# Relus, memory rows and tile values at other steps and engines in a fused chunk attention and feed-forward kernel

## The chip, the cores and the metric

The kernel runs on one core of a Trainium2 chip. Time is device time in microseconds (us). The kernel before was timed six times: the median is 212.51 us, the runs lie between 211.23 and 214.04 us.

## The reference, cut to what matters

Attention goes over chunks of 32 queries; each chunk sees 16 keys to its left, its own 32, 8 to its right, and 8 memory rows. Its output is normalised and goes through a two-layer perceptron with a residual.

```python
# q, k, v: (4, 8, 768, 64); mem_k, mem_v: (4, 8, 8, 64)
for c in range(24):                                   # chunks of 32
    k_ctx = k[:, :, max(0, 32*c - 16) : min(768, 32*c + 40)]
    k_full = concat([mem_k, k_ctx]); v_full = concat([mem_v, v_ctx])
    a = softmax(scale * q_c @ k_full.T)
    out[:, :, c_start:c_end] = a @ v_full
x = out.transpose(0, 2, 1, 3).reshape(4, 768, 512)
xn = (x - mean(x)) / sqrt(var(x) + 1e-6) * g_ln       # over the 512
y = x + maximum(xn @ w_ch1, 0) @ w_ch2                # 512 -> 2048 -> 512
```

## The kernel before, in words

**Tiles and units.** A tile is 128 rows of `x` (one batch has six, there are 24). Three tiles make a unit: units 0 and 1 hold batch 0, units 2 and 3 batch 1 and so on, counted in the tiles of the perceptron. The perceptron of unit `u` runs while the attention of the next unit's tiles is made.

**Steps.** A unit has 28 steps, written out by the loop at lines 901 to 923. In steps 0 to 15, `up` multiplies the three turned tiles `xT` by one 128-wide slice `hc` of the first weight (four matmuls of 384 columns) into one of four PSUM buffers `mm`, which rotate; a relu then moves it to `rT`. Line 435 says on which engine: for units 2 to 7 (`PAIRED`) VectorE takes `hc` 3, 5, 8, 11, 13 and 15, ScalarE the rest. In steps 16 to 27, `down` and `paired` multiply `rT` by the second weight. In units 2 to 7, `down` makes the third tile in steps 16 to 19 and `finish` (line 483) empties its `mm` buffer; `paired` makes the first two tiles from sums and differences of blocks, which VectorE prepares in `mixed_r` (lines 503 to 512, operation at line 491). The fourth product of `paired` goes into the buffer that `finish` empties.

**What is planned beside it.** `at(u, step, fn, ...)` puts other work behind the perceptron's work of a step. An engine takes its instructions in the order in which they are written; there is no other scheduler. `attend` plans three attention tiles: `scores` (line 326) and `soften` (the exponential on ScalarE, line 337), then `weigh` (probabilities by values, line 354), `gather` (VectorE, lines 363 to 373, divides and takes the mean), `norm` (line 376) one step later, `turn_x` (two or more steps later) and `stats` (line 381, ScalarE). Tiles listed in `ON_PE` are turned by four TensorE transposes and a VectorE copy (lines 404 and 409), the others by a DMA transpose on SyncE's queue (line 399).

**Memory rows.** `v_mem` (line 142) copies the eight memory value rows of a batch to the partitions 96 to 103 of the value buffer `V`, four groups at a time. For batches 2 and 3 ScalarE does it at steps 17, 21 and 24 of units 1 and 3.

**Loads.** GpSimd's queue starts nearly all loads, in the order of the program: the values of unit 0 between quarters of the first weight (`w1c`) and of the second (`w2c`), lines 659 to 687. `mix` (line 304) is a VectorE copy of a landed block of keys or queries (`st` to `iv`), which is then turned by TensorE (batches 0 and 1) or by DMA (`cross`, batches 2 and 3) and put in its place by `spread`. Unit 0 begins as a written-out list (lines 697 to 767) and goes on with the steps from 10.

Of the kernel before, what the change touches and what calls it, by code (L numbers as in the profile page):

```python
# [15 lines left out]
def kernel(  # L16
# [20 lines left out]
    GW = 4 * W  # L37
    VW = 80
    HD = 65
    ON_PE = (0, 1, 2, 3, 4, 5, 8)  # L40
    NEG = -30000.0

    ctx.enter_context(tc.manual_schedule())
# [43 lines left out]
    def slot(kind):  # L87
        lst = {"att": att, "mm": mm}[kind]
        turn[kind] = (turn[kind] + 1) % len(lst)
        return lst[turn[kind]]  # L90
# [4 lines left out]
    def free(ap, off, pattern, parts=None):  # L95
        p = list(ap.ap[0]) if parts is None else [ap.ap[0][0], parts]
        return bass.AP(tensor=ap.tensor, offset=ap.offset + off, ap=[p] + [list(x) for x in pattern])

    def as16(t):
        return t.bitcast(FP16)  # L100

    def copy(eng, out, in_):
        if eng is nc.scalar:
            eng.copy(out=out, in_=in_)  # L104
        else:
            eng.tensor_copy(out=out, in_=in_)  # L106

    dve, act, pool = nc.vector, nc.scalar, nc.gpsimd
    ring = {}

    def pick(lst, key):
        key = (id(lst),) + key
        if key not in ring:
            ring[key] = ring.setdefault(("n", id(lst)), 0) % len(lst)
            ring[("n", id(lst))] += 1
        return lst[ring[key]]
# [168 lines left out]
    def mix_q(b, blk, half, eng):  # L285
        rows = slice(64 * half, 64 * half + 64)
        s, o = pick(st, ("b", b, blk, 1))[rows, :], pick(iv, ("b", b, blk, 1))[rows, :]
        copy(eng, free(o, 0, [[64, 2], [128, 8], [1, 64]]), s)
# [13 lines left out]
    def mix(b, blk, which, eng):  # L302
        s, o = pick(st, ("b", b, blk, which)), pick(iv, ("b", b, blk, which))
        copy(eng, free(o, 0, [[64, 2], [128, 8], [1, 64]]), s)
# [40 lines left out]
    def values(b, t):  # L345
        weigh(b, t)
        gather(b, t)

    def weigh(b, t):
        p = value_slot[b, t] = slot("att")  # L350
        for par in range(2):
            for j in range(4):
                for gg in range(2):
                    nc.tensor.matmul(  # L354
                        out=p[64 * gg : 64 * gg + 64, par, 128 * j : 128 * j + HD],
                        lhsT=AT[t % 3][:, par, gg, j, :],
                        rhs=V[b % 2][:, 2 * t + gg, 4 * par + j, 0:HD],
                        start=(j == 0), stop=(j == 3), tile_position=(0, 64 * gg),
                    )

    def gather(b, t):
        p, r, x = value_slot[b, t], rec[t % 2], xs[(NT * b + t) % 9]
        nc.vector.reciprocal(out=r, in_=free(p, 64, [[128, 8]]))  # L363
        nc.vector.scalar_tensor_tensor(  # L364
            out=x.rearrange("p (h d) -> p h d", h=8),
            in0=free(p, 0, [[128, 8], [1, 64]]), scalar=1.0,
            in1=free(r, 0, [[1, 8], [0, 64]]),
            op0=ALU.mult, op1=ALU.mult, accum_out=tot[t],
        )
        nc.vector.tensor_scalar(  # L370
            out=nmean[t], in0=tot[t], scalar1=-1.0 / 512, scalar2=None, op0=ALU.mult
        )

    def norm(b, t, gb=gb):
        i = NT * b + t
        nc.vector.scalar_tensor_tensor(  # L376
            out=xn[i % 4], in0=xs[i % 9], scalar=nmean[t], in1=gb, op0=ALU.add, op1=ALU.mult,
        )
# [16 lines left out]
    def turn_x(b, t):  # L395
        i = NT * b + t
        dst = xT[(i // 3) % 2][:, :, 128 * (i % 3) : 128 * (i % 3) + 128]
        if i not in ON_PE:
            nc.sync.dma_start_transpose(out=dst, in_=xn[i % 4])
            return  # L400
        p = slot("att")
        pv = as16(p[:, 0, :])
        for dt in range(4):
            nc.tensor.matmul(
                out=pv[:, 128 * dt : 128 * dt + 128],
                lhsT=xn[i % 4][:, 128 * dt : 128 * dt + 128], rhs=identity,
                is_transpose=True, start=True, stop=True,
            )
        nc.vector.tensor_copy(out=dst, in_=free(pv, 0, [[128, 4], [1, 128]]))
# [10 lines left out]
    def relu(eng, o, p):  # L420
        if eng is nc.scalar:
            nc.scalar.activation(out=o, in_=p, func=ACTF.Relu)  # L422
        else:
            nc.vector.tensor_scalar(out=o, in0=p, scalar1=0.0, scalar2=None, op0=ALU.max)  # L424

    def up(u, hc, lo=0, n=3):
        p = slot("mm")[:, 0 : 128 * n]
        c, i = hc // 4, hc % 4
        for dt in range(4):
            nc.tensor.matmul(  # L430
                out=p, lhsT=free(w1c[c][:, dt, :], i, [[4, 128]]),
                rhs=xT[u % 2][:, dt, 128 * lo : 128 * (lo + n)],
                start=(dt == 0), stop=(dt == 3),
            )
        on_dve = hc in (3, 5, 8, 11, 13, 15) if u in PAIRED else hc % 2 == 0
        relu(dve if on_dve else act, rT[c][:, i, 128 * lo : 128 * (lo + n)], p)

    def up_two(u, c, engs):

        for m, eng in enumerate(engs):  # L440
            p = slot("mm")
            for k_ in range(2):
                for dt in range(4):
                    nc.tensor.matmul(
                        out=p[:, 256 * k_ : 256 * k_ + 256],
                        lhsT=free(w1c[c][:, dt, :], 2 * m + k_, [[4, 128]]),
                        rhs=xT[u % 2][:, dt, 0:256],
                        start=(k_ == 0 and dt == 0), stop=(k_ == 1 and dt == 3),
                    )
            relu(eng, rT[c][:, 2 * m : 2 * m + 2, 0:256], free(p, 0, [[256, 2], [1, 256]]))  # L450

    def up_tile(u, c, i, eng):
        p = slot("mm")
        for k_ in range(4):
            for dt in range(4):
                nc.tensor.matmul(
                    out=p[:, 128 * k_ : 128 * k_ + 128],
                    lhsT=free(w1c[c][:, dt, :], k_, [[4, 128]]),
                    rhs=xT[u % 2][:, dt, 128 * i : 128 * i + 128],
                    start=(k_ == 0 and dt == 0), stop=(k_ == 3 and dt == 3),  # L460
                )
        pair = rT[c][:, :, 128 * i : 128 * i + 128], free(p, 0, [[128, 4], [1, 128]])
        if eng is None:
            return pair
        relu(eng, *pair)
# [22 lines left out]
    PAIRED = range(2, 8)  # L488
# [269 lines left out]
    total(cnt[:, 2:3], 96, W)  # L758
    nc.vector.tensor_tensor(out=cnt[:, 1:2], in0=cnt[:, 1:2], in1=cnt[:, 2:3], op=ALU.add)
    up_tile(0, 0, 1, act)  # L760
    up_two(0, 1, (dve, act))
    values(0, 2)
    norm(0, 2)
    up_two(0, 2, (act, act))
    turn_x(0, 2)
    mix_q(0, 1, 1, dve)
    mix(0, 2, 0, dve)
    plan = {}

    def at(u, step, fn, *args):  # L770
        plan.setdefault((u, step), []).append((fn, args))
# [11 lines left out]
    def value(tiles, s1, u, also=()):  # L783
# [9 lines left out]
        for n, i in enumerate(tiles):  # L793
            b, t = divmod(i, NT)
            at(u, s1 + 1, norm, b, t)
            at(u, s1 + n + (2, 3, 4)[(i in ON_PE) + (i == 8)], turn_x, b, t)
            at(u, s1 + n + 2, stats, b, t)
# [5 lines left out]
    def attend(i, s0, s1, s2, u):  # L803

        score((i, i + 1), s0, u)
        value((i,), s1, u, (i + 2,))
        value((i + 1, i + 2), s2, u)
# [62 lines left out]
    for b in (2, 3):  # L870
        u = 2 * b - 1
        w = u - 1
        for blk in range(3):
            if b == 3 and blk == 0:
                at(w - 1, 0, pace, 0, 0)
            at(w - 1, 0 if b == 3 else 21, load_pair, b, blk)
        at(w, 0, mem_cols, b, pool)
        at(w - 1, 24, pace_x, 6 * b - 4)
        for g in range(NG):
            at(w - 1, 24 + g // 4, load_v, b, g)  # L880
        for i in range(3):
            at(w - 1, (17, 21, 24)[i], v_mem, b, 4 * i, 4 * i + 4, act)
        for blk in range(3):
            for which in range(2):
                at(w, (3, 9, 18)[blk] + which, mix, b, blk, which, dve)
                at(w, (7, 18, 23)[blk] + 3 * which, cross, b, blk, which)
        at(w, 18, spread, b, 0, dve, act)
        at(w, 27, spread, b, 1, dve, act)
        at(u, 9, spread, b, 2, dve, act)
        attend(6 * b, 2, 8, 14, u)  # L890
    for b in (1, 2, 3):
        attend(6 * b + 3, 0, 6, 12, 2 * b)

    for n in range(8):
        at(1, 16 + n, mixed_w, n % 2, n // 2)
# [5 lines left out]
    for u in range(8):  # L901
        for step in range(U):
# [9 lines left out]
            elif u == 0:  # L912
                c, i = divmod(step - 16, 3)
                down(u, i, c)
            elif u not in PAIRED:
                i, c = divmod(step - 16, 4)
# [37 lines left out]
```

## Time and profile before

| | us |
|---|---|
| median of six runs | 212.51 |
| the profiled execution's own time | 212.71 |
| its span, first to last instruction | 210.9 |
| TensorE busy in the span | 199.4 |
| VectorE busy | 157.8 |
| ScalarE busy | 123.1 |
| GpSimd busy | 107.6 |

The granted TensorE clock was 1.00 in every slice. A timeline row gives the start, the length, the engine, the line, the operation, output and input, how many instructions are merged in it, and in brackets the idle time of the engine before it with what ended that. A busy matmul row ends with the drain of its last matmul, so two rows can touch although matmuls were started late; how late shows when the starts are counted. A row of engine times by stretch gives the stretch, the busy time and the number of instructions of an engine, the granted clock, the share of the DMA engines and GB/s.

### The profile page before, as it was taken

To read this page: it belongs to the slowest core of one execution; us is meant where nothing else is said; L and a number is where in the kernel's file an instruction comes from. 1 tells how busy PE (TensorE), PEld (TensorE's weight loads), DVE (VectorE), ACT (ScalarE), POOL (GpSimd) and SP (SyncE) were. 2 spreads that over 40 slices of the span, in tenths; PEclk is the share of its full clock that TensorE was granted. 3 is DMA by queue.
4 is the path that set the end of the run, shared out by engine and by line. 5 is a ranking of instruction groups with operands and counts; after the bars stand their busy time and mean duration, and the time that the engine had idled before them with its cause. 6 is when DMAs were issued, how large, how long until landed. Compare 5 with 4: busy or idle time off the path is not lost.

```text
span 210.9 us, 5313 instructions
## 1 busy us (share of the span) xinstructions
PE 199.4 (95%) x2052; PEld 135.2 (64%) x2052; DVE 157.8 (75%) x402; ACT 123.1 (58%) x243; POOL 107.6 (51%) x187
## 2 busy tenths in 40 slices
PE   7778699999999999999999999999999999999992
PEld 2457585556665567587657766686658765777581
DVE  6878567597979948997579778995789458863663
ACT  2777368627796997625879885528850684024100
POOL 7955598979789799725884991400040012100000
PEclk9999999999999999999999999999999999999999
DMA  5999999999999999999994999388013210320012
GB/s 152 201 195 190 207 182 182 205 116 240 179 93 125 204 170 148 141 214 193 172 157 97 98 199 184 72 177 148 9 24 99 99 29 1 103 99 0 3 50 99
DMA packets 72499, 27.72 MB, mean 131 GB/s; under 512 B 60569, under 2 KB 68505, under 8 KB 72474
## 3 DMA queue, kind: packets, MB, share of 16 engines
q0 software_dynamic: 46304, 14.71, 66.1%
q1 hardware_dynamic: 26026, 12.41, 26.8%
q10 hardware_dynamic: 144, 0.26, 0.6%
q8 instruction: 16, 0.26, 0.5%
q14 instruction: 9, 0.07, 0.1%
HBM read 30.28 MB, written 6.29 MB: 173 GB/s over the span
## 4 chain that ended last, share of the span: by engine, by line
PE 62%; DVE 11%; ACT 5%; issue 2%; DVEq 0%
PE mm L430 31%; PE mm L517 13%; PE mm L474 12%; PE att L354 3%; PE att L326 3%; DVE xs L364 2%; DVE SA L491 2%; DVE xn L376 2%; ACT AT L337 2%; ACT KT L104 1%; DVE osb L483 1%; DVE osb L533 1%; ACT rT L422 1%; DVE rT L424 1%; DVE KT L106 1%
## 5 line engine op out<-in xcount | busy, mean ns | idle before, releaser
L430 PE MATMUL mm<-xT,w1c 128*128 128x384 f16 x464 | 81.4, 327 | 0.8 <-ACT rT L422 0.6
L430 PEld LDWEIGHTS <-w1c 128*128 128x128 f16 x464 | 51.1, 115 | 22.2 <-issue 1.3
L422 ACT ACTIVATE rT<-mm 128x384 f16<-128x384 f32 (+1 forms) x76 | 37.2, 502 | 37.7 <-PE mm L430 31.1
L424 DVE TENSOR_SCALAR rT<-mm 128x384 f16<-128x384 f32 (+1 forms) x49 | 27.5, 562 | 26.0 <-PE mm L430 25.3
L474 PE MATMUL mm<-w2c,rT 128*128 128x512 f16 x192 | 44.6, 380 | 0.0
L137 POOL DMA_DIRECT2D V<-in_v_dram x48 | 37.6, 795 | 4.9 <-issue 1.4
L337 ACT ACTIVATE AT<-att,band 104x512 f16<-104x512 f32 x48 | 31.6, 689 | 4.5 <-PE att L326 4.4
L387 POOL TENSOR_SCALAR veps<-sq 128x1 f32<-128x1 f32 x24 | 7.8, 325 | 45.6 <-ACT junk L381 42.9
L474 PEld LDWEIGHTS <-rT 128*128 128x128 f16 x192 | 18.2, 98 | 19.7 <-DVE rT L424 0.8
L517 PEld LDWEIGHTS <-SA 128*128 128x128 f16 x192 | 18.8, 98 | 3.0 <-issue 0.8
L381 ACT ACTIVATE junk<-xs,nmean 128x512 f16<-128x512 f32 x24 | 17.3, 721 | 5.1 <-DVE rec L363 2.1
L517 PE MATMUL mm<-T,SA 128*128 128x256 f16 x144 | 17.0, 273 | 0.4 <-DVE osb L483 0.4
L364 DVE SCALAR_TENSOR_TENSOR xs<-att,rec 128x512 f32<-128x512 f32 x24 | 16.6, 691 | 0.8
L391 POOL TENSOR_TENSOR rstd<-veps,mhalf 128x1 f32<-128x1 f32 x24 | 16.1, 672 | 2.0
L376 DVE SCALAR_TENSOR_TENSOR xn<-xs,nmean,gb 128x512 f16<-128x512 f32 x23 | 16.8, 755 | 0.3
L517 PEld LDWEIGHTS <-rT 128*128 128x128 f16 x144 | 14.1, 98 | 2.9 <-issue 0.4
L123 POOL DMA_DIRECT2D st<-in_q_dram x24 | 13.3, 567 | 2.4 <-DMA st<-in_k_dram 1.4
L129 POOL DMA_DIRECT2D st<-in_k_dram x22 | 13.3, 615 | 2.1 <-DMA w1c<-in_moe_w_ch_dram 2.0
L104 ACT COPY V<-memv 8x2560 f16<-8x2560 f16 x6 | 13.8, 2320 | 0.1
L517 PE MATMUL mm<-w2c,rT 128*128 128x256 f16 x96 | 12.4, 273 | 0.0
L106 DVE COPY iv<-st 128x1024 f16<-128x1024 f16 (+1 forms) x22 | 10.6, 495 | 1.6 <-DMA st<-in_k_dram 1.4
L354 PEld LDWEIGHTS <-AT 104*64 104x64 f16 x384 | 7.7, 111 | 6.4 <-issue 4.4
(105 smaller groups left out, 241.2 us busy)
## 6 DMA issues: line engine op xcount, KB each, us to landing
out_dram<-osb SPq DMA_DIRECT2D x23, 256.0 KB, 2.4
V<-in_v_dram POOLq DMA_DIRECT2D x40, 96.0 KB, 6.1
st<-in_k_dram POOLq DMA_DIRECT2D x22, 128.0 KB, 5.3
w1c<-in_moe_w_ch_dram POOLq DMA_DIRECT2D x4, 512.0 KB, 9.3
w2c<-in_moe_w_ch_dram POOLq DMA_DIRECT2D x4, 512.0 KB, 8.3
st<-in_q_dram POOLq DMA_DIRECT2D x28, 64.0 KB, 4.3
st<-in_q_dram POOLq DMA_DIRECT2D x8, 128.0 KB, 7.6
V<-in_v_dram POOLq DMA_DIRECT2D x8, 80.0 KB, 5.6
```

Source lines behind the costliest of these rows:

```text
L104: eng.copy(out=out, in_=in_)
L137: nc.gpsimd.dma_start(out=V[b % 2][lo:hi, g, :, 0:64], in_=dram(v, b * H * HS + (64 * g - 16 + lo) * D, [[64, hi - lo], [HS, H], [1, 64]]),)
L337: nc.scalar.activation(out=free(AT[t % 3], 32 * c, [[64, 16], [1, 32]]), in_=free(p, 4 * c, [[64, 16], [1, 4], [8, 8]], W), func=ACTF.Exp, ...
L364: nc.vector.scalar_tensor_tensor(out=x.rearrange("p (h d) -> p h d", h=8), in0=free(p, 0, [[128, 8], [1, 64]]), scalar=1.0, in1=free(r, 0, ...
L376: nc.vector.scalar_tensor_tensor(out=xn[i % 4], in0=xs[i % 9], scalar=nmean[t], in1=gb, op0=ALU.add, op1=ALU.mult,)
L381: nc.scalar.activation(out=junk, in_=xs[(NT * b + t) % 9], func=ACTF.Square, bias=nmean[t], scale=1.0, accum_out=sq[t],)
L391: nc.gpsimd.tensor_tensor(out=rstd[(NT * b + t) % 9], in0=veps[t % 3], in1=mhalf, op=ALU.pow)
L422: nc.scalar.activation(out=o, in_=p, func=ACTF.Relu)
L424: nc.vector.tensor_scalar(out=o, in0=p, scalar1=0.0, scalar2=None, op0=ALU.max)
L430: nc.tensor.matmul(out=p, lhsT=free(w1c[c][:, dt, :], i, [[4, 128]]), rhs=xT[u % 2][:, dt, 128 * lo : 128 * (lo + n)], start=(dt == 0), st ...
L474: nc.tensor.matmul(out=p, lhsT=rT[c][:, k_, 128 * i : 128 * i + 128], rhs=w2c[c][:, k_, :], start=(c == 0 and k_ == 0), stop=(c == 3 and k ...
L517: nc.tensor.matmul(out=p, lhsT=left(h)[:, k_, :], rhs=right(h)[:, k_, :], start=(h == 0 and k_ == 0), stop=(h == 1 and k_ == 3),)
```

## The change

It has five parts. (1) Tile 7 (batch 1, second tile) is turned by TensorE, at step 19 of unit 1, and no longer by DMA at step 18. (2) In units 2 to 7, VectorE takes the relus 1, 2, 4, 5, 8, 10 in even units and 3, 4, 6, 7, 10, 11 in odd ones; ScalarE has the last four or five. (3) The memory rows of batches 2 and 3 are copied by VectorE at steps 0, 1 and 2 of units 2 and 4, and no longer by ScalarE. (4) The second and third tile of an attention group are weighed one step earlier (13 for 14, 11 for 12), and with them their gathering, norm, turning and stats. (5) In unit 0, tile 2's values stand ahead of the second quarter of the first weight; both relus of that quarter are ScalarE's; the third quarter is split around tile 2's turning.

```diff
-    ON_PE = (0, 1, 2, 3, 4, 5, 8)
+    ON_PE = (0, 1, 2, 3, 4, 5, 7, 8)
...
-        on_dve = hc in (3, 5, 8, 11, 13, 15) if u in PAIRED else hc % 2 == 0
+        on_dve = hc in ((1, 2, 4, 5, 8, 10), (3, 4, 6, 7, 10, 11))[u % 2] if u in PAIRED else hc % 2 == 0
...
-        for m, eng in enumerate(engs):
+        for m, eng in engs:
...
     up_tile(0, 0, 1, act)
-    up_two(0, 1, (dve, act))
     values(0, 2)
+    up_two(0, 1, ((0, act), (1, act)))
     norm(0, 2)
-    up_two(0, 2, (act, act))
+    up_two(0, 2, ((0, act),))
     turn_x(0, 2)
+    up_two(0, 2, ((1, act),))
     mix_q(0, 1, 1, dve)
     mix(0, 2, 0, dve)
...
         for i in range(3):
-            at(w - 1, (17, 21, 24)[i], v_mem, b, 4 * i, 4 * i + 4, act)
+            at(w, i, v_mem, b, 4 * i, 4 * i + 4, dve)
...
-        attend(6 * b, 2, 8, 14, u)
+        attend(6 * b, 2, 8, 13, u)
     for b in (1, 2, 3):
-        attend(6 * b + 3, 0, 6, 12, 2 * b)
+        attend(6 * b + 3, 0, 6, 11, 2 * b)
```

## The prediction, made before the changed kernel was run

> **What bounds the kernel now.** I read the page's busy shares and slices first, then TensorE's busy time by stretch, then the timeline at each place where TensorE started late.
>
> ```profile
> PE 199.4 (95%) x2052; PEld 135.2 (64%) x2052; DVE 157.8 (75%) x402; ACT 123.1 (58%) x243; POOL 107.6 (51%) x187
> ...
> PE   7778699999999999999999999999999999999992
> ```
> ```profile
> 47.75:73.32 25.57, 25.41 (x250) 1.00 1.29 168
> 73.32:96.06 22.74, 22.52 (x233) 1.00 1.58 170
> 96.06:118.98 22.92, 22.59 (x235) 1.00 0.93 143
> 118.98:141.59 22.61, 22.40 (x233) 1.00 1.26 154
> 141.59:164.46 22.87, 22.56 (x234) 1.00 0.36 70
> 164.46:186.71 22.25, 22.25 (x234) 1.00 0.19 55
> ```
>
> TensorE is the bound from unit 1 on (the rows are units 1 to 6). Unit 6 has no idle time and takes 22.25; units 2 to 5 do the same products in 22.61 to 22.92. What they have over unit 6, 0.49 + 0.67 + 0.36 + 0.62 = 2.1 us, is about all that a better order can win there. The holes lie in unit 0 (first nine slices). The places in unit 4 and unit 3:
>
> ```profile
> 134.05 0.55 DVE L424 TENSOR_SCALAR rT<-mm 128x384 f16<-128x384 f32 x1
> ...
> 135.82 1.91 PE L517 MATMUL mm<-T,SA 128*128 128x256 f16 x16
> ...
> 137.14 0.75 DVE L483 SCALAR_TENSOR_TENSOR osb<-mm,rstd,xs 128x512 f32<-128x512 f32 x1
> ...
> 137.94 1.03 PE L517 MATMUL mm<-T,SA 128*128 128x256 f16 x8 [0.21 <-DVE osb L483]
> ```
> ```profile
> 103.45 3.44 PE L430 MATMUL mm<-xT,w1c 128*128 128x384 f16 x20
> ...
> 105.28 1.48 ACT L104 COPY KT<-rawk 128x352 f16<-128x352 f16 x2
> ...
> 106.66 0.49 ACT L422 ACTIVATE rT<-mm 128x384 f16<-128x384 f32 x1
> ...
> 107.20 0.81 PE L430 MATMUL mm<-xT,w1c 128*128 128x384 f16 x4 [0.32 <-ACT rT L422]
> ```
>
> Undisturbed, 24 matmuls of 256 columns take 2.63 us in the chain of waits (0.11 each) and 64 of 384 columns 10.40 (0.163 each). So the 16 from 135.82 should be followed at 137.57; 137.94 is 0.37 late, because VectorE, behind its relu 15, emptied the buffer late. The 20 from 103.45 should be followed at 106.70; 107.20 is 0.50 late, because relu 10 sat behind ScalarE's key copies. The same counts give 0.39 in unit 2 (92.41) and 0.51 in unit 5 (152.69).
>
> **Relus and the step of the values (odd units 3 and 5).** VectorE keeps six relus. Relu 10 passes to it, behind the norm that ends at 106.0; relus 10 and 11 at 0.48 apiece (start to start) end near 107.0. The weighing, 0.63 for two tiles, now stands before `up` 14, which needs relu 10's buffer at 106.7 + 0.63 = 107.35: in time. Added to ScalarE before the key copies is relu 8 (0.49): it starts at 102.85 and ends before the exponential that can begin at 103.56. After the copies and one stats (0.9), relus 12 to 15 run from 107.8 to 109.7; `down`'s last quarter needs them at 111.2. Cover 1.5 us. On SyncE's queue the tiles' DMA transposes move up a step with their norms; GpSimd's loads that wait for one (at 115.85) come sooner, and nobody waits for them. Won: 0.50 + 0.51.
>
> **The same in even units 2 and 4, with the memory rows.** VectorE loses relus 11, 13 and 15 late in the unit (3 x 0.48) and gets the copies at steps 0 to 2:
>
> ```profile
> L104 ACT COPY V<-memv 8x2560 f16<-8x2560 f16 x6 | 13.8, 2320 | 0.1
> L106 DVE COPY V<-memv 8x2560 f16<-8x2560 f16 x4 | 3.3, 824 | 0.1
> ```
>
> ScalarE is rid of 13.9 us that no TensorE wait ends on. VectorE gets 3 x 0.83 per unit. Queue in unit 4, the tighter one: VectorE is free at 119.94; copy, relu 1 (ready 121.0), copy, relu 2, copy, `mix`, relu 4, `mix`, relu 5 end at 120.8, 121.5, 122.3, 122.8, 123.6, 124.1, 124.6, 125.1 and 125.6. TensorE wants relu 2's buffer at step 6 (123.4) and relu 5's at step 9 (126.2): cover 0.6 both times. Then gather (1.05), norm (0.67), relus 8 and 10, two `mix`, two gathers at 129.2 and two norms to 132.6, against 133.26 before. Up to the start of `finish` it was 3.9 from there; without relu 15 it is 3.4. So `finish` ends at 132.6 + 3.4 + 0.75 = 136.8, and is wanted at 137.57: the late start goes. Unit 2 gives an end 1.1 earlier than before by the same sum. Won: 0.39 + 0.37. Relu 15 on ScalarE, behind two stats, ends near 133.5; the last quarter of `down` wants it at 134.0. Cover 0.5: what is late next.
>
> The Trainium skill speaks against the copies (SBUF — State Buffer, Who interferes with whom): a VectorE copy in a two-port mode and a GpSimd instruction exclude each other for a whole instruction. GpSimd issues value loads of 0.77 us through both windows. By that rule two copies could be held 1.5 us and three 2.3, which eats the 0.6. The rows: the four copies of this shape took 823 to 828 ns, also beside such issues; the 1024-wide `iv` copies took 0.42, and 0.56 to 0.77 where issues flanked them. I take 0 to 0.3 a copy, and keep 0.77 for the range.
>
> Units 6 and 7 have no memory copies and no late start that the relus decide; the relus there have a matmul group of 0.65 for an instruction of 0.49. I put 0, and for the range up to 0.3 against.
>
> **Tile 7 turned by TensorE (unit 1).**
>
> ```profile
> 62.53 2.77 PE L474 MATMUL mm<-w2c,rT 128*128 128x512 f16 x12
> ...
> 64.83 1.41 DVE L376 SCALAR_TENSOR_TENSOR xn<-xs,nmean,gb 128x512 f16<-128x512 f32 x2
> ...
> 65.13 0.61 PE L233 MATMUL mm<-identity,iv 128*128 128x128 f16 x8
> ...
> 65.60 1.21 SPq L399 DMA_TRANSPOSE xT<-xn  x1
> ```
>
> At step 19 TensorE arrives at 65.13, before its key transposes. Tile 7's norm, the first of two from 64.83, ends at 65.58, as the DMA transpose that waited for it shows. TensorE will stand until about 65.62, then four transposes: at 43.30 such a group, after the same wait, was followed by the next product 0.23 later. So 65.85 for 65.13: 0.72 lost, behind which all of TensorE's queue stands. The skill (TensorE: Matmul & The Clock Gate, Part 4: PE-mode transpose) gives about 275 ns for one in a kernel; four would make 1.1, and 1.6 lost. The rows have 0.22 to 0.24 for four back to back, so I take that. VectorE's added copy (0.42) and the one turn more of the two attention buffers have over a microsecond of cover before unit 2 needs `xT` (73.15, last copy at 71.06). SyncE loses one transpose; its next entry comes at 68.47.
>
> **Unit 0.**
>
> ```profile
> 23.12 1.94 PE L444 MATMUL mm<-xT,w1c 128*128 128x256 f16 x16 [1.26 <-DMA w1c<-in_moe_w_ch_dram]
> ...
> 25.87 1.95 PE L456 MATMUL mm<-xT,w1c 128*128 128x128 f16 x32 [0.58 <-DVE xT L409]
> ...
> 43.86 0.72 DVE L106 COPY iv<-st 128x1024 f16<-128x1024 f16 x1
> ```
>
> The values of tile 2 need a load started at 11.34 that lands 9.2 later, at 20.5; the weight's quarter lands at 19.2. TensorE will stand for 1.0 at 19.5, but the third quarter lands only at 23.1, and by 20.5 + 0.4 + 1.7 = 22.6 it is through: nothing lost. Then the norm is done before 23.1, the second half covers the turning, and the product at 25.87 starts 0.8 earlier. This does not reach the end of the unit: the `mix` at 43.86 needs a load issued at 34.66 that took 9.2, so 43.84, and from it VectorE is busy without a hole to 47.70, when the last `finish` frees the buffer for TensorE's 47.75. GpSimd's loads had something in flight all the way (2.4 us for each 512 KB), so earlier products bring none of them forward. I take 0; up to 0.6 if that landing moves.
>
> **The sum.** 212.71 - 0.50 - 0.51 - 0.39 - 0.37 + 0.72 = 211.66 against the profiled execution, which is 0.20 above the median: 211.5.
>
> **Rivals.** *The even units keep their late starts* because the copies push VectorE back by as much as the relus free: 0.76 not won, 212.3. For it: cover of only 0.6. *Unit 0 passes its 0.6 on*, or tile 7 finds its norm ready (0.5): 210.9, with both 210.4. Against: the landing at 43.84. *Slower: the port lock in units 2 and 4.* If each copy is held by a GpSimd issue (0.77), relu 5 ends at 127.9 and TensorE waits 1.7 at step 9, twice: 211.5 + 0.76 + 3.4 = 215.7. It decides from 0.2 a copy on, and makes the kernel slower than before from about 0.25: then 0.76 is not won, the other parts leave 0.3, and 2 x (3 x 0.25 - 0.6) uses it up. Against: 823 ns beside GpSimd's issues.
>
> **How the numbers follow.** The forecast 211.5 has 0.5, the first rival 0.2, the second 0.17, the slow one 0.13. The range goes from 210.0 (second rival with both halves, and 0.4 for the scatter of a median, where single runs lie 1.3 below theirs) to 213.7 (first rival, 0.9 more for tile 7 at the skill's price, 0.5 for units 6 and 7 and scatter); it leaves out most of the slow case. About 1%, 2.1 us, is what a measurement of this kernel can tell from no change: faster than that 0.15 (half the second rival and the edge of the forecast), within 0.70, slower 0.15.
>
> **What would show it.** Right: no late start at the fourth `paired` product of units 2 and 4 nor at `up` 14 of units 3 and 5, and these units at 22.2 to 22.5; a wait of TensorE on `xn` in unit 1, which grows by 0.7; unit 1 beginning at 47.7. Wrong: relus 1, 2 or 5 with TensorE waiting on them, memory copies above 1 us, TensorE waiting for ScalarE's relu 15, or unit 1 beginning before 47.3.

## The result, and the profile after

The changed kernel took 211.21 us (median of 33 runs, 209.77 to 212.94); the kernel before, run beside it, 212.48 us (70 runs). The ratio is 0.9938, with a 95% interval of 0.9922 to 0.9954: 1.3 us faster, within 1.0 and 1.7. The forecast was 211.5, 1.0 us faster. Medians, here and below, are over all runs, while ratios leave out the slow runs, those over 1.5% above the fastest of their kernel, so the two can differ by some tenths.

The busy shares and the slices of the changed kernel:

```profile
PE 198.4 (95%) x2056; PEld 135.4 (65%) x2056; DVE 164.1 (78%) x408; ACT 110.7 (53%) x238; POOL 109.0 (52%) x187
...
PE   6778979999999999999999999999999999999992
```

VectorE has 6 us more to do, ScalarE 12 us less, and neither sum explains the time. TensorE's time by stretch does (unit 1 from its second product on, then units 2 to 6; columns as before):

```profile
47.84:73.99 26.15, 25.65 (x253) 1.00 1.38 156
73.99:96.23 22.24, 22.24 (x233) 1.00 1.56 163
96.23:118.48 22.25, 22.25 (x235) 1.00 1.06 164
118.48:140.83 22.35, 22.35 (x235) 1.00 1.30 155
140.83:163.07 22.24, 22.24 (x234) 1.00 0.27 69
163.07:185.32 22.25, 22.25 (x234) 1.00 0.19 55
```

Units 2 to 5, counted in the same way from first product to first product, took 22.75, 22.92, 22.61 and 22.87 before: 91.15 in all. Now they take 89.08, and each has come down to what unit 6 takes. Unit 1, from its second product, took 73.15 - 47.75 = 25.40 and now takes 26.15. Unit 0 ends 0.09 later, the rest of the kernel after unit 6 takes 0.06 more. -2.07 + 0.75 + 0.09 + 0.06 = -1.17, the difference of the two spans (210.93 and 209.76).

Timeline of unit 4 of the changed kernel, at the place where the fourth product of `paired` was late:

```profile
135.59 2.78 PE L517 MATMUL mm<-T,SA 128*128 128x256 f16 x24
136.04 0.75 DVE L483 SCALAR_TENSOR_TENSOR osb<-mm,rstd,xs 128x512 f32<-128x512 f32 x1
```

All 24 matmuls are one row now: `finish` (L483) ends at 136.79, and the last eight want its buffer at 135.59 + 16 x 0.11 = 137.3. The same in unit 3, at `up` 14:

```profile
103.58 3.44 PE L430 MATMUL mm<-xT,w1c 128*128 128x384 f16 x20
...
106.10 1.02 DVE L424 TENSOR_SCALAR rT<-mm 128x384 f16<-128x384 f32 x2
...
106.96 0.70 PE L354 MATMUL att<-V,AT 104*64 104x65 f16 x32
...
107.59 1.49 PE L430 MATMUL mm<-xT,w1c 128*128 128x384 f16 x8
```

Relus 10 and 11 end at 107.12 on VectorE; `up` 14 begins at 107.59, right behind the weighing. What the change costs is seen in unit 1, at tile 7:

```profile
64.92 1.41 DVE L376 SCALAR_TENSOR_TENSOR xn<-xs,nmean,gb 128x512 f16<-128x512 f32 x2
...
65.73 0.40 PE L404 MATMUL att<-identity,xn 128*128 128x128 f16 x4 [0.35 <-DVE xn L376]
...
65.96 0.61 PE L233 MATMUL mm<-identity,iv 128*128 128x128 f16 x8
```

TensorE stands for tile 7's norm, and its key transposes begin at 65.96, where they began at 65.13.

### The profile page after: what moved, and what is told of

Read it like the earlier page. It is cut to its first block, busy times and chain, and to the rows that moved or that the text cites. A ratio compares the mean times of both kernels' runs of the same rounds, so it can differ in the third digit from the quotient of the medians.

```text
span 209.8 us, 5308 instructions
## 1 busy us (share of the span) xinstructions
PE 198.4 (95%) x2056; PEld 135.4 (65%) x2056; DVE 164.1 (78%) x408; ACT 110.7 (53%) x238; POOL 109.0 (52%) x187
## 4 chain that ended last, share of the span: by engine, by line
PE 72%; DVE 6%; ACT 2%; issue 1%; DVEq 0%
PE mm L430 35%; PE mm L517 16%; PE mm L474 14%; PE att L354 3%; PE att L326 3%; ACT AT L337 1%; DVE xs L364 1%; DVE osb L533 1%; DVE xn L376 1%; DVE osb L483 1%; PE att L233 1%; PE att L404 1%; PE mm L233 0%; ACT rT L422 0%; DVE rec L363 0%
## 5 line engine op out<-in xcount | busy, mean ns | idle before, releaser
L422 ACT ACTIVATE rT<-mm 128x384 f16<-128x384 f32 (+1 forms) x77 | 38.0, 498 | 44.6 <-PE mm L430 41.0
L137 POOL DMA_DIRECT2D V<-in_v_dram x48 | 38.4, 809 | 7.0 <-DMA w1c<-in_moe_w_ch_dram 2.2
L424 DVE TENSOR_SCALAR rT<-mm 128x384 f16<-128x384 f32 (+1 forms) x48 | 26.7, 560 | 14.2 <-PE mm L430 13.0
L337 ACT ACTIVATE AT<-att,band 104x512 f16<-104x512 f32 x48 | 31.1, 687 | 3.3 <-PE att L326 3.3
L387 POOL TENSOR_SCALAR veps<-sq 128x1 f32<-128x1 f32 x24 | 7.2, 299 | 44.5 <-ACT junk L381 22.6
L391 POOL TENSOR_TENSOR rstd<-veps,mhalf 128x1 f32<-128x1 f32 x24 | 15.6, 652 | 2.0
L129 POOL DMA_DIRECT2D st<-in_k_dram x22 | 12.8, 590 | 1.7 <-DMA w1c<-in_moe_w_ch_dram 1.4
L104 ACT COPY KT<-rawk 128x352 f16<-128x352 f16 (+1 forms) x12 | 8.9, 790 | 6.0 <-DMA rawk<-iv 6.0
L104 ACT COPY KT<-mm 128x176 f16<-128x176 f16 (+2 forms) x28 | 6.7, 309 | 10.0 <-PE mm L233 6.8
```

Source lines behind the costliest of these rows:

```text
L137: nc.gpsimd.dma_start(out=V[b % 2][lo:hi, g, :, 0:64], in_=dram(v, b * H * HS + (64 * g - 16 + lo) * D, [[64, hi - lo], [HS, H], [1, 64]]),)
L337: nc.scalar.activation(out=free(AT[t % 3], 32 * c, [[64, 16], [1, 32]]), in_=free(p, 4 * c, [[64, 16], [1, 4], [8, 8]], W), func=ACTF.Exp, ...
L391: nc.gpsimd.tensor_tensor(out=rstd[(NT * b + t) % 9], in0=veps[t % 3], in1=mhalf, op=ALU.pow)
```

## The experiments

All kernels were timed beside the kernel before, which took 212.5 to 212.8 us. Gains in us between two experiments are taken from their ratios.

**The parts of the change, one at a time.** The relus alone:

```diff
-        on_dve = hc in (3, 5, 8, 11, 13, 15) if u in PAIRED else hc % 2 == 0
+        on_dve = hc in ((1, 2, 4, 5, 8, 10), (3, 4, 6, 7, 10, 11))[u % 2] if u in PAIRED else hc % 2 == 0
```

> The kernel before with the new list of relus alone. Theory (the late starts are VectorE's relus 13 and 15 in even units and ScalarE's relu 10 in odd ones): all four go, units 2 to 5 take 22.2 to 22.5 us each, 1.6 to 1.8 us faster than the kernel before, ratio near 0.992. Rival (the values one step earlier are needed for it, since in odd units relu 10 on VectorE then comes just behind the norm and relu 14's buffer is wanted 0.6 earlier): only the even units win, 0.8 us, ratio 0.996.

Measured: 209.97 us, ratio 0.9887 (0.9835 to 0.9938). TensorE's time by stretch, units 2 to 5:

```profile
72.25:94.49 22.24, 22.24 (x233) 1.00 1.73 178
94.49:116.74 22.25, 22.25 (x234) 1.00 1.08 152
116.74:138.99 22.25, 22.25 (x235) 1.00 1.33 160
138.99:161.23 22.24, 22.24 (x234) 1.00 0.36 69
```

All four late starts are gone with the relus alone: 91.15 - 88.98 = 2.2 us, more than the 1.3 that the whole change wins. The rival, that odd units need the earlier values too, falls.

The earlier values alone (`attend(6 * b, 2, 8, 13, u)` for 14, `attend(6 * b + 3, 0, 6, 11, 2 * b)` for 12):

> The kernel before with the values of the second and third tile one step earlier, and nothing else. Theory (each late start is a matter of a few tenths: in odd units the weighing of 0.63 us then stands before product 14, which waited 0.5 for relu 10; in even units VectorE's gathers begin 0.65 earlier, so that relu 15 and the emptying of the buffer, 0.38 late, come in time): the step alone removes the four late starts as well, units 2 to 5 take 22.2 to 22.5 us, ratio to the kernel before 0.992. Rival (only the relus' engines matter): no difference, ratio 0.999 to 1.001, the four late starts stay.

Measured: 210.73 us, ratio 0.9921 (0.9903 to 0.9940). Units 2 to 5:

```profile
72.21:94.77 22.56, 22.41 (x233) 1.00 1.64 179
94.77:117.29 22.52, 22.51 (x234) 1.00 0.98 152
117.29:139.54 22.25, 22.25 (x235) 1.00 1.55 152
139.54:161.87 22.33, 22.33 (x234) 1.00 0.34 72
```

Most of it goes this way too; 0.3 stays in unit 2, where the third run of eight in `paired` still starts 0.31 late, and 0.3 in unit 3, in two small waits. The rival, that only the relus' engines matter, falls. The relus and the step are two remedies for one complaint. Together, without the other three parts:

> The kernel before with the new relus and the values one step earlier, without the memory rows, tile 7 and unit 0. Theory (relus and step each remove the same late starts): nothing is left for the second of them, units 2 to 5 at 22.25 us, ratio 0.988 to 0.991 as with the relus alone. Rival (they add up): ratio near 0.981.

Measured: 210.13 us, ratio 0.9880 (0.9853 to 0.9907). They do not add up; all of units 2 to 6 are at 22.25. (The granted clock of this profile was down to 0.5 and 0.7 in the fourth and fifth of its forty slices, in unit 0; in units 1 to 6 it was 1.00.)

The memory rows alone (`at(w, i, v_mem, ..., dve)` for `at(w - 1, (17, 21, 24)[i], v_mem, ..., act)`):

> The kernel before with the memory rows of batches 2 and 3 on VectorE at steps 0 to 2 of units 2 and 4, and nothing else. Theory (VectorE is idle for 2.4 us there, which is what three copies take; ScalarE's copies held nobody): no difference, ratio 0.999 to 1.001, copies of 0.82 to 1.2 us. Rival (the port lock with GpSimd's loads): copies above 1.3 us, products of units 2 and 4 that wait for relu 3 or 5, 1 to 3 us slower.

Measured: 212.87 us, ratio 1.0019 (1.0000 to 1.0039): nothing or a little slower. The units in which ScalarE lost its copies, 1 and 3, gained nothing by it: 25.74 for 25.40, with a wait that is shown further down, and 22.90 for 22.92. The copies took 0.81 to 1.08 us on VectorE, and unit 2 has 23.18 in place of 22.75, because its last `down` product waited 0.5 for relu 15, which VectorE now does later.

The new order of unit 0 alone:

> The kernel before with the new order of unit 0 alone. Theory (the end of unit 0 hangs on a load of keys that lands at 43.8 to 43.9 and on VectorE's full queue behind it): no difference, ratio 0.999 to 1.001; products of steps 10 and 11 start 0.8 to 1.7 earlier, and the second product of unit 1 still starts at 47.7 to 47.9. Rival (the earlier products are passed on): 0.5 us faster, ratio 0.9975, second product of unit 1 at 47.2.

Measured: 212.53 us, ratio 0.9993 (0.9963 to 1.0022). No difference is seen, but the interval holds the rival's 0.9975 too, so the time alone does not decide. Nor does this profile: its granted clock was down to 0.5 and 0.7 in the fourth and fifth of its forty slices, the very place that was changed, and the products at step 10 started at 26.39, where they started at 25.87 before. The keys landed at 44.30 and the second product of unit 1 started at 48.16: 3.86 after the landing, as in the kernel before (47.75 - 43.84 = 3.91). All profiles but the one of relus with earlier values (49.38) together speak for the theory: with the new order of unit 0 that product started at 46.35 to 48.16 in five kernels, without it at 46.69 to 48.24 in seven.

**Tile 7.** The changed kernel without it (`ON_PE = (0, 1, 2, 3, 4, 5, 8)`):

> The changed kernel with tile 7 turned by DMA as before. Theory (TensorE stands for tile 7's norm at step 19 and does four transposes more): 0.7 to 0.8 us faster than the changed kernel, ratio to the kernel before near 0.990; no wait of TensorE on xn in unit 1, and the key transposes of step 19 at 65.2 in place of 65.96. Rival (something else in unit 1 is late anyway, so that the 0.8 is only moved): within 0.2 us of the changed kernel, and unit 2 still starts 0.8 after its start in the kernel before.

Measured: 210.32 us, ratio 0.9891 (0.9856 to 0.9926), against 0.9938 for the changed kernel: about 1.0 us faster, with an interval of 0.2 to 1.8. From the second product of unit 1 to unit 2 it took 25.53, not 26.15. The rival, that the loss is only moved, falls.

Tile 7 turned by TensorE, but a step later:

```diff
-            at(u, s1 + n + (2, 3, 4)[(i in ON_PE) + (i == 8)], turn_x, b, t)
+            at(u, s1 + n + (2, 3, 4)[(i in ON_PE) + (i in (7, 8))], turn_x, b, t)
```

> The changed kernel with tile 7 turned by TensorE at step 20 in place of 19. Theory (of the 0.84 us that unit 1 lost, 0.5 is the wait for the norm and 0.23 the transposes): 0.5 us faster than the changed kernel, no wait on xn, ratio to the kernel before near 0.991. Rival (TensorE's transposes cost what the skill's 275 ns gives, 1.1 us): less than 0.2 us faster than the changed kernel.

Measured: 211.00 us, ratio 0.9930 (0.9901 to 0.9959): 0.2 us better than at step 19, not 0.5. TensorE's timeline in unit 1:

```profile
66.48 0.39 PE L404 MATMUL att<-identity,xn 128*128 128x128 f16 x4
66.70 1.03 PE L474 MATMUL mm<-w2c,rT 128*128 128x512 f16 x4
...
69.92 0.61 PE L233 MATMUL att<-order,iv 128*128 128x128 f16 x8 [0.24 <-DVE xT L409]
```

There is no wait on the norm, and the four transposes cost 66.70 - 66.48 = 0.22; the 1.1 of the rival was an estimate, four times the 275 ns that the Trainium skill gives for one in a kernel (TensorE: Matmul & The Clock Gate, Part 4: PE-mode transpose). But TensorE now stands at 69.92 for VectorE to copy tile 7 out of the attention buffer that the query transposes want; counted by the starts that is 0.41, so unit 1 took 26.04, only 0.11 less. And in this profile unit 2 took 22.62, where the changed kernel had 22.25. VectorE's memory copies were longer there:

```profile
74.86 1.23 DVE L106 COPY V<-memv 8x2560 f16<-8x2560 f16 x1
...
76.71 1.17 DVE L106 COPY V<-memv 8x2560 f16<-8x2560 f16 x1
...
78.50 1.17 DVE L106 COPY V<-memv 8x2560 f16<-8x2560 f16 x1
```

In unit 2 of the changed kernel the three took 0.82 each. GpSimd issued value loads through all three copies here, and only at the end of the third there. The products at steps 6, 8 and 9 started 0.11, 0.13 and 0.15 late. Why GpSimd came to these loads at another time was not tested. The time is about as the rival said (the interval of the difference also holds the theory's 0.5), the reason is another.

**The memory rows on a busy VectorE.** Relus and memory rows, the values at their old steps:

> The kernel before with the new relus and the memory rows on VectorE; the values stay at their old steps. Theory (VectorE's queue in units 2 and 4 is at its limit with the copies, and without the earlier gathers relus 5 to 10 still come in time by some tenths): no late start above 0.3 us, units 2 and 4 at 22.25 to 22.6, ratio near 0.989 to 0.991 as with the relus alone. Rival (the copies need the earlier step): the fourth paired product of units 2 and 4 is late again by 0.3 to 0.5 each, 0.8 us slower than the relus alone.

Measured: 211.43 us, ratio 0.9962 (0.9937 to 0.9987), 1.6 us slower than with the relus alone. Neither theory gave this. Unit 4 took 23.08. Its timeline:

```profile
119.92 1.17 DVE L106 COPY V<-memv 8x2560 f16<-8x2560 f16 x1
121.12 0.56 DVE L424 TENSOR_SCALAR rT<-mm 128x384 f16<-128x384 f32 x1
121.70 1.17 DVE L106 COPY V<-memv 8x2560 f16<-8x2560 f16 x1
...
127.08 0.81 PE L430 MATMUL mm<-xT,w1c 128*128 128x384 f16 x4 [0.18 <-DVE rT L424]
```

Copies of 0.90, 1.17 and 1.17 us push back relus 1 to 8; TensorE starts late by 0.22 at step 6 and 0.35 at 127.08 (step 12), and by smaller amounts between, all through buffers of `up`, and not at the fourth `paired` product that the rival named. Unit 2 of the same profile, whose three copies took 0.82 each, had 22.25: there the copies cost nothing, and in unit 4 an excess of 0.77 in the three goes with 0.83 of lost time (by the prediction unit 4's queue is also the tighter one; how much of the loss is due to that was not tested). It is the slow case of the prediction in small. In the changed kernel, with the values earlier, unit 4 took 22.35 with 0.48 of excess, and with tile 7 at step 20 unit 2 took 22.62 with 1.1: the earlier step pays for most of a long copy, not for all of it.

The same copies at steps 3 to 5 of units 3 and 5 (`at(u, 3 + i, v_mem, ..., dve)`):

> The kernel before with the new relus and the memory rows on VectorE, but at steps 3 to 5 of units 3 and 5. Theory (a copy is lengthened only where GpSimd issues loads back to back: it does so through steps 0 to 10 of unit 4, and not at all in unit 5): all three copies of unit 5 take 820 to 830 ns, unit 4 is back at 22.25, ratio 0.988 to 0.991. In unit 3, where GpSimd issues key and query loads, single copies of 0.9 to 1.2 us. Rival (the copies are slow because of VectorE's own queue or of the loads' traffic, not of GpSimd's issues): copies of unit 5 above 0.9 us, and late starts move to units 3 and 5.

Measured: 211.80 us, ratio 0.9960 (0.9935 to 0.9985). Unit 4 was at 22.25, and the copies of unit 5, where GpSimd issues nothing, took 816 to 824 ns. But those of unit 3 took 823 to 826 too, beside GpSimd's issues, and units 3 and 5 took 23.11 and 23.00. Unit 5:

```profile
145.34 0.82 DVE L106 COPY V<-memv 8x2560 f16<-8x2560 f16 x1
...
152.05 1.00 DVE L424 TENSOR_SCALAR rT<-mm 128x384 f16<-128x384 f32 x2
152.64 0.81 PE L430 MATMUL mm<-xT,w1c 128*128 128x384 f16 x4 [0.59 <-DVE rT L424]
```

The late start moved there, as the rival said, but not for its reason: the copies had their plain length, and 2.5 us of them is simply more than VectorE's queue has room for ahead of relu 10. That GpSimd lengthens copies wherever it issues, as the theory had it for unit 3, falls with the 823 to 826 ns there.

**Two tries for a faster kernel.** Relus, unit 0's order, and the held key copy of unit 0 further back in VectorE's queue (`at(0, 25, mix, 1, 0, 0, dve)` behind tile 5's turning, for step 23):

> The kernel before with the new relus and the new order of unit 0, and one thing more: the key copy of batch 1 that waits for its load at the end of unit 0 stands behind tile 5's turning instead of before tile 4's. Theory (this copy, held by the load that lands at 43.8 to 44.0, holds VectorE's queue and with it the last three emptied buffers): the second product of unit 1 starts 0.2 to 0.4 earlier against the landing than with the old place, no wait of VectorE for that load in front of tile 4's xT, ratio near 0.988. Rival (the queue behind is full in any order): second product as late after the landing as before (3.9 us), time as with the relus alone.

Measured: 209.49 us, ratio 0.9877 (0.9839 to 0.9914): not to be told from the relus alone. In its profile the keys landed at 42.19 and the second product of unit 1 started at 46.35, 4.16 later. VectorE did not wait for that load, as the theory said, but the first `finish` then waited 0.43 for TensorE's product, and the end came no sooner after the landing. The rival's time stands, and the theory, that this copy holds the queue, falls.

Relus, earlier values, and relu 15 of unit 1 on VectorE:

```diff
-... if u in PAIRED else hc % 2 == 0
+... if u in PAIRED else hc % 2 == 0 or (u == 1 and hc == 15)
```

> As the one with new relus and earlier values, and relu 15 of unit 1 on VectorE in place of ScalarE. Theory (the 0.33 us that TensorE waits in unit 1 for the last exponential of tile 8 is one relu in front of it on ScalarE): no wait there, 0.3 us faster than without it. Rival (VectorE's gathers and norms behind the relu come 0.5 later, and tile 7's DMA transpose with them, which already lands close to unit 2's start): unit 2 starts as late as before or later, with TensorE waiting for xT.

Measured: 211.39 us, ratio 0.9916 (0.9889 to 0.9942), 0.8 us slower than without it, though the two intervals overlap. The wait for the last exponential (0.33) went, and a larger one came:

```profile
66.02 1.21 SPq L399 DMA_TRANSPOSE xT<-xn  x1
...
74.05 0.81 PE L430 MATMUL mm<-xT,w1c 128*128 128x384 f16 x4 [1.11 <-DVE T L491]
```

Counted from unit 1's second product, tile 7's DMA transpose was issued at 18.77 (66.02 - 47.25) and not at 17.85 as before (65.60 - 47.75). Half of that had been lost earlier in unit 1, at a copy of keys; 0.4 is the relu's. Unit 2's first product stood for 1.1. The profile names VectorE's last operation before it, which that product does not read; that it was the transposed tile is argued from the kernels with the memory rows alone and with relus and earlier values, where the same product carries the name:

```profile
73.57 0.81 PE L430 MATMUL mm<-xT,w1c 128*128 128x384 f16 x4 [0.17 <-DMA xT<-xn]
```
```profile
75.79 0.81 PE L430 MATMUL mm<-xT,w1c 128*128 128x384 f16 x4 [0.84 <-DMA xT<-xn]
```

In the first the transpose issued at 65.69 was read at 73.57, nearly 8 us later; in the second, issued at 67.24, it was read at 75.79, 8.6 later. Where nothing waited, unit 2 began 7.55 after the issue.

## Why the prediction was right, point by point

**The four late starts** were the gain, as forecast: 1.77 by the sum, 2.07 measured. The missing 0.3 is in smaller late starts that the sum did not count: in the kernel before, the products at step 3 of units 3 and 5 started 0.19 and 0.15 late and two of unit 2 together 0.12, while the changed kernel has only 0.10 left, in unit 4. That these units would come down to unit 6's 22.25 was in the first view of the prediction (2.1), and that was the better number.

**Which part wins it** was put too broadly. The prediction credited relus and earlier values together. The runs show that the relus alone are enough and the earlier values nearly so. The earlier values are then needed for what the memory rows cost.

**The memory rows.** ScalarE's 13.9 us were rightly put at nothing. For VectorE the sum had 0.83 each and 0 to 0.3 for GpSimd. The copies of the changed kernel in unit 4, and the relu at the end of that queue:

```profile
119.61 0.82 DVE L106 COPY V<-memv 8x2560 f16<-8x2560 f16 x1
...
121.27 0.95 DVE L106 COPY V<-memv 8x2560 f16<-8x2560 f16 x1
...
122.83 1.17 DVE L106 COPY V<-memv 8x2560 f16<-8x2560 f16 x1
...
125.36 0.54 DVE L424 TENSOR_SCALAR rT<-mm 128x384 f16<-128x384 f32 x1
```

The excess is 0, 0.13 and 0.35. Relu 5 ends at 125.90; step 9 wants its buffer at 124.53 + 8 x 0.163 = 125.83, and started 0.10 late. The cover of 0.6 was used up to the last tenth, as the slow rival's deciding point, 0.2 a copy, has it: on the average the copies had 0.16. So two of the prediction's own signs of being wrong came, in small: a copy above 1 us, and TensorE waiting for relu 5. That it stayed small was in part luck. The third copy lies above the 0 to 0.3 that was taken, and the average depends on when GpSimd comes to its loads: with tile 7 a step later it was 0.37 in unit 2, and the unit took 0.37 more. Where the queue had less cover (relus and memory rows alone) unit 4 lost 0.8.

**Tile 7** was put at 0.72 and cost 0.75; taking it out gave 0.62 in unit 1 of the profile and about 1.0 in time, with an interval (0.2 to 1.8) that holds both. The four transposes took 0.22 to 0.23. What the prediction left out is what the move saves: it counted when SyncE issues, not when the DMA transpose lands. That transpose lands so near to unit 2's start that TensorE waited 0.17, 0.84 and perhaps 1.11 us for it in three of the eleven profiles that have it. The move pays a fixed 0.75 for an occasional wait.

**Unit 0** was put at 0, and no gain was seen, though the interval of its own experiment leaves room for 0.8. The chain was partly wrong on the way. In the kernel before, the landing at 43.84 held nobody yet, for VectorE was busy with two norms until 43.91:

```profile
42.50 1.41 DVE L376 SCALAR_TENSOR_TENSOR xn<-xs,nmean,gb 128x512 f16<-128x512 f32 x2
```

In the changed kernel it did. Timeline rows of the changed kernel:

```profile
27.76 0.74 DVE L106 COPY iv<-st 128x1024 f16<-128x1024 f16 x1 [3.03 <-DMA st<-in_k_dram]
...
28.56 0.62 PE L233 MATMUL mm<-identity,iv 128*128 128x128 f16 x8 [1.11 <-DVE iv L106]
...
43.93 0.73 DVE L106 COPY iv<-st 128x1024 f16<-128x1024 f16 x1 [0.34 <-DMA st<-in_k_dram]
...
47.84 0.81 PE L430 MATMUL mm<-xT,w1c 128*128 128x384 f16 x4 [0.28 <-DVE osb L483]
```

In this execution the loads came a microsecond sooner, TensorE stood 0.28 and not 1.0 for the values, and the products at step 10 began at 24.15 where they began at 25.87. Most of this was lost at 28.56 to an earlier load of keys, which the prediction had not named, and the last 0.3 at 43.93, which it had. Whether the end of unit 0 hangs on that landing stays open: it came 3.7 to 4.5 after it in all profiles but one (5.0), but all loads of unit 0 shift together, and with the held copy moved back the end came no sooner.

**Relu 15 on ScalarE**, "what is late next", did not become late: it ended at 132.81 in unit 4 (forecast 133.5). Unit 6 took 22.25 before and after, and the rest behind it 0.06 more.

## What to carry to other kernels

Count the starts of a full engine, unit by unit, against a unit that runs without a hole: the difference is what a new order can win, and it held here to a few hundredths of a microsecond per unit. Moving work off an engine that nobody waited for won nothing here, and the engine that got it paid from the cover of everything queued behind it. The bundle won 1.3 us, while one line of it, the list of relus, won 2.4 (1.3 to 3.5) alone, and the earlier values alone 1.7: time the parts one by one. When a turning or a copy is moved to another engine, count the landing of the transfer that it replaces, not its issue alone.

## What the runs showed of the hardware that was not expected

- The loads of unit 0 come at quite different times from execution to execution: the second key load of batch 1 landed between 42.19 and 44.34 us in the profiles of this study, and the second product of unit 1 began between 46.35 and 49.38. This scatter is larger than the whole gain, and no experiment shows a part that moves it. The granted clock is not all of it: it was down to between 0.5 and 0.7 for one or two slices of unit 0 in three of the thirteen profiles, the one with 49.38 among them, but 48.24 and a landing at 44.27 came with 1.00 throughout.
- A VectorE copy of 8 x 2560 took 0.82 us with no GpSimd issue beside it (unit 5 of the kernel with the copies in odd units), and from 0.82 to 1.23 beside GpSimd's load issues, with 1.17 in most of the long ones. The longest hold seen was 0.41, about half of an issue of 0.77; an issue that began during a copy of 1.17 took 1.04 in place of 0.77. Many copies beside issues stayed at 0.82 (unit 3 of the same kernel), and what decides between the two was not tested.
- Four 128 x 128 transposes in TensorE's queue cost 0.22 to 0.23 us from their start to the next product's.
